# Eight turns of q and k moved from TensorE to DMA transposes, the last unit's halves in tiles of their own, and a new order of the steps

## The chip, the cores and the metric

One core of one Trainium2 chip. The time is the device time of one execution in microseconds (us). In what follows PE is the matrix engine (TensorE), DVE the vector engine, ACT the scalar engine, POOL GpSimd, and SP the engine that issues most DMAs. Every run has a state: it is called slow if it is more than 1.5% above the fastest run of the same kernel, and verdicts use only the other, fast, runs.

## The reference

Attention with a bias by distance, a local window of 96 keys and 8 global keys; then a feed-forward block on the result, whose nonlinearity is `h * softmax(h)` followed by a layer norm.

```python
# q, k, v: (4, 8, 768, 64); x: (3072, 512); w_in: (512, 1024); w_out: (1024, 512)
keep = is_global | ((rel >= 0) & (rel < 96))
scores = scale * q @ k.T - slope[h] * dist          # where keep, else -1e9
x = (softmax(scores) @ v)                           # heads side by side, 512 wide
h = x @ w_in
solu = h * softmax(h)
out = ((solu - mean) / sqrt(var + 1e-6) * g_ln) @ w_out
```

## The kernel before

The 3072 tokens are twelve units of 256 tokens (three per batch). For each unit, q and k are loaded, cast to 16 bits and turned, so that the head's 64 numbers lie on partitions; then come scores (`sc`, and `gs` for the global keys), exponentials (`pt`), sums (`lb`), values (`pa`), and the feed-forward block in two groups of 128 tokens: first layer (`ph`), exponential (`e`), product (`un`), a turn of `un` (mostly a DMA transpose, `uT`), second layer (`po`), scaling (`osb`), store. A list of steps, `ORDER`, fixes the order in which each engine gets its instructions; every engine works its own list in order, as the traces show (ACT stood for 2.21 us at one `osb` here, SP for 22.6 us at one transpose in experiment 2).

The turn of q and k, and the copy that puts the turned tile in token order:

```python
def small(shape, dt, name):                    # PSUM: two buffers for everything small
    return psum.tile(shape, dt, name=name, tag="small", bufs=2)

def turn(name, u):
    src = held.pop((name + "16", u))
    t = held["p" + name, u] = small([P, NR, P], FP16, name + "turned")
    for r in range(NR):                        # NR = 8
        nc.tensor.transpose(out=t[:, r], in_=src[:, r]..., identity=held["ident"])

def evac_qk(engine, name, u):
    t = held[name + "T", u] = attn.tile([P, NPAIR, UQ], FP16, name=name + "T", ...)
    cast(engine, t.rearrange("p g (i r) -> p g i r", r=NR),
         held.pop(("p" + name, u)).rearrange("p r (i g) -> p g i r", g=NPAIR))
```

The last unit's first layer is done in halves of the 1024 columns, and both halves are in one accumulator tile:

```python
def ff_in(t, h=None):
    if ("ph", t) not in held:
        held["ph", t] = big("ph")...           # one tile for both halves
    for j in range(NCC):
        for fh in (0, 1) if h is None else (h,):
            nc.tensor.matmul(out=held["ph", t][:, ts(fh, 512)], ...)
```

and the order near the end has `A:11:0:0 E:11:0:0 U:11:0:0 A:11:0:1 E:11:0:1`: A is the first layer, E the exponential, U the product. So the second half is written after the first half's readers.

The softmax here doesn't subtract the row's maximum and nothing guards it: scores larger than these inputs give would overflow.

## Time and profile before

| | before |
|---|---|
| median of the timed runs | 174.66 us (174.57 to 175.02) |
| span in the profile | 173.2 us |
| PE, DVE, ACT, POOL busy | 154.9, 127.3, 144.5, 91.4 us |
| moved by DMA | 34.35 MB |

The lines of the page that carry the argument are in the prediction below. These are the only two PE waits of over 0.1 us between 60 and 120 us (columns: engine, tile and line that waited, what it waited for, total us, times, longest):

```profile
PE gs L353 <- ACT osb L536: 1.3, 1, 1.3
PE ph L446 <- DVE xT L430: 0.7, 1, 0.7
```

### The profile page before, as it was taken

Reading aid. Unit: us, or ns where it says so; the run is one execution under the profiler, and the core shown is the slowest. Engines: PE = TensorE matmul, PEld = TensorE weight load, DVE = VectorE, ACT = ScalarE, POOL = GpSimd, SP = SyncE. Lnnn points to the kernel's source line nnn. Section 1 sums busy time; section 2 is a strip of 40 time slices with the busy share of each in tenths; the row PEclk is TensorE's granted clock in tenths of the full one; section 3 lists DMA queues with packets and bytes.
Section 4 is the critical chain, followed back from the end, with each engine's and each line's share of the span. In section 5 each row is a group of like instructions: output and inputs, shape, how many; then the busy total and the mean of one; then the engine's idle time right before and its main releaser. Section 6 shows DMA issues by size and latency. Waiting matters only on the chain.

```text
span 173.2 us, 4093 instructions
## 1 busy us (share of the span) xinstructions
PE 154.9 (89%) x1551; PEld 86.1 (50%) x1551; DVE 127.3 (73%) x200; ACT 144.5 (83%) x232; POOL 91.4 (53%) x195
## 2 busy tenths in 40 slices
PE   0179599899999989997999999999999958998997
PEld 0156375655654545436455655555545634454443
DVE  5079978999899989929989899869837672475310
ACT  5959999899999997769999899999895566796540
POOL 5276809300814998987288987882210001464760
PEclk9999759999999999999999999999999999999999
DMA  4999999999999998689999692398753530055354
GB/s 138 309 346 310 328 255 244 256 354 287 312 341 162 221 109 166 111 249 234 360 206 155 147 217 98 121 264 224 167 140 74 169 125 0 0 164 139 68 162 198
DMA packets 52532, 34.35 MB, mean 198 GB/s; under 512 B 43169, under 2 KB 43681, under 8 KB 52513
## 3 DMA queue, kind: packets, MB, share of 16 engines
q1 hardware_dynamic: 48784, 27.14, 63.9%
q0 software_dynamic: 1984, 5.77, 13.9%
q10 hardware_dynamic: 1744, 1.18, 2.5%
q8 instruction: 12, 0.20, 0.5%
q14 instruction: 8, 0.06, 0.1%
HBM read 23.07 MB, written 6.29 MB: 169 GB/s over the span
## 4 chain that ended last, share of the span: by engine, by line
PE 66%; POOL 10%; DVE 5%; DMA 5%; ACT 5%; issue 5%; SPq 4%; POOLq 0%; DVEq 0%; ACTq 0%
PE ph L446 21%; PE po L522 20%; PE lb L393 5%; PE pa L412 4%; PE warm L230 4%; SPq L157 4%; PE sc L324 3%; DMA q<-in_q_dram 3%; PE qturned L301 3%; POOL gw L594 2%; DMA v<-in_v_dram 2%; PE kturned L301 2%; DVE q L140 2%; ACT pt L333 2%; PE pa L422 1%
## 5 line engine op out<-in xcount | busy, mean ns | idle before, releaser
L446 PE MATMUL ph<-w_in,xT 128*128 128x512 f16 x192 | 44.9, 379 | 3.1 <-DVE un L468 2.3
L522 PE MATMUL po<-gw,uT 128*128 128x512 f16 x192 | 44.5, 379 | 0.0
L333 ACT ACTIVATE pt<-sc 128x896 f16<-128x896 f32 (+1 forms) x48 | 40.0, 871 | 2.2 <-PE sc L324 2.0
L468 DVE SCALAR_TENSOR_TENSOR un<-e,ph 128x1024 f16<-128x1024 f16 (+1 forms) x26 | 29.1, 1135 | 8.5 <-ACT e L460 7.6
L340 DVE TENSOR_TENSOR pt<-pt,mask 128x896 f16<-128x896 f16 (+1 forms) x48 | 28.3, 614 | 5.5 <-ACT pt L333 5.5
L446 PEld LDWEIGHTS <-xT 128*128 128x128 f16 x192 | 17.8, 98 | 24.0 <-issue 2.6
L460 ACT ACTIVATE e<-ph 128x1024 f16<-128x1024 f32 (+1 forms) x26 | 24.8, 955 | 4.5 <-PE ph L446 2.8
L522 PEld LDWEIGHTS <-uT 128*128 128x128 f16 x192 | 17.9, 98 | 20.9 <-issue 0.5
L477 ACT ACTIVATE sq<-un 128x1024 f16<-128x1024 f16 (+1 forms) x26 | 25.7, 990 | 2.0 <-DVE un L468 1.8
L497 POOL TENSOR_SCALAR w<-s,w 128x1 f32<-128x1 f32 x22 | 6.8, 311 | 32.3 <-ACT sq L477 30.6
L324 PE MATMUL sc<-qT,kT 64*128 64x128 f16 (+2 forms) x256 | 15.9, 246 | 3.0 <-ACT kT L138 1.8
L430 DVE TENSOR_TENSOR xT<-pa,rlb 128x1024 f16<-128x1024 f32 x12 | 14.6, 1221 | 2.9 <-ACT rlb L402 1.6
L301 PE MATMUL kturned<-ident,k 128*128 128x128 f16 x96 | 8.8, 246 | 8.0 <-POOL k L142 8.0
L495 POOL TENSOR_SCALAR w<-mean,w 128x1 f32<-128x1 f32 x24 | 14.5, 605 | 2.4
L499 POOL TENSOR_TENSOR rs<-w,neghalf 128x1 f32<-128x1 f32 x24 | 14.6, 610 | 2.0
L140 DVE COPY kT<-kturned 128x1024 f16<-128x1024 f16 x9 | 11.0, 1222 | 6.0 <-PE kturned L301 6.0
L534 DVE TENSOR_SCALAR osb<-po,rs 128x512 f32<-128x512 f32 (+1 forms) x15 | 10.7, 711 | 5.8 <-DMA out_dram<-osb 3.0
L401 ACT ACTIVATE rlb<-lb 128x1024 f32<-128x1024 f32 x12 | 12.4, 1032 | 3.0 <-PE lb L393 2.8
L536 ACT ACTIVATE osb<-po,rs 128x512 f32<-128x512 f32 (+1 forms) x11 | 7.1, 650 | 8.5 <-PE po L522 4.5
L324 PEld LDWEIGHTS <-kT 64*128 64x128 f16 x256 | 9.3, 100 | 8.3 <-issue 4.6
L402 ACT ACTIVATE rlb<-rlb 128x1024 f32<-128x1024 f32 x12 | 12.7, 1057 | 0.4
L301 PEld LDWEIGHTS <-k 128*128 128x128 f16 x96 | 7.1, 111 | 10.1 <-POOL k L142 8.2
(88 smaller groups left out, 230.2 us busy)
## 6 DMA issues: line engine op xcount, KB each, us to landing
out_dram<-osb SPq DMA_DIRECT2D x11, 512.0 KB, 2.9
q<-in_q_dram SPq DMA_DIRECT2D x19, 256.0 KB, 5.2
k<-in_k_dram SPq DMA_DIRECT2D x18, 256.0 KB, 5.3
v<-in_v_dram SPq DMA_DIRECT2D x16, 256.0 KB, 6.3
v<-in_v_dram POOLq DMA_DIRECT2D x7, 256.0 KB, 5.0
k<-in_k_dram POOLq DMA_DIRECT2D x6, 256.0 KB, 8.2
w_out<-in_moe_w_out_dram SPq DMA_DIRECT2D x3, 512.0 KB, 6.1
q<-in_q_dram POOLq DMA_DIRECT2D x5, 256.0 KB, 8.6
```

Of the source, the lines that this page charges most:

```text
L301: nc.tensor.transpose(out=t[:, r], in_=src[:, r].rearrange("p m d -> p (m d)"), identity=held["ident"])
L324: nc.tensor.matmul(out=sc[:, m, o : o + e - a], lhsT=held["kT", u - s + j // 2][r, g, ts(j % 2, P)], rhs=qT[r, g, a:e], start=True, stop=True,
L333: nc.scalar.activation(out=pt[:, :, 0:w], in_=held.pop(("sc", u, g))[:, :, 0:w], func=AF.Exp, scale=inv_sqrt_d)
L340: nc.vector.tensor_tensor(out=pt[:, :, 0:w], in0=pt[:, :, 0:w], in1=held["mask"][:, g, :, o : o + w], op=ALU.mult)
L430: nc.vector.tensor_tensor(out=xT.rearrange("p g (r i) -> p g r i", r=2), in0=held.pop(("pa", u)).rearrange("p g (i r) -> p g r i", r=2), i ...
L446: nc.tensor.matmul(out=held["ph", t][:, ts(fh, 512)], lhsT=held["xT", t[0]][:, j, ts(t[1], P)], rhs=held["w_in"][:, j, ts(fh, 512)], start ...
L460: nc.scalar.activation(out=held["e", t][:, f], in_=held["ph", t][:, f], func=AF.Exp, accum_out=s0)
L468: nc.vector.scalar_tensor_tensor(out=held["un", t][:, f], in0=held["e", t][:, f], scalar=1.0, in1=held["ph", t][:, f], op0=ALU.mult, op1=A ...
L477: nc.scalar.activation(out=sq[:, f], in_=held["un", t][:, f], func=AF.Square, accum_out=s2)
L495: eng.tensor_scalar(out=w2, in0=mean, scalar1=mean, scalar2=w1, op0=ALU.mult, op1=ALU.subtract)
L499: eng.tensor_tensor(out=rs, in0=w3, in1=held["neghalf"], op=ALU.pow)
L522: nc.tensor.matmul(out=held["po", t], lhsT=held["uT", t][:, c, :], rhs=held["gw"][:, c, :], start=(c == 0), stop=(c == NFC - 1),)
```

## The change

It has three parts. Five turns of k (units 7 to 11) and three of q (units 9 to 11) become DMA transposes, into SBUF tiles, with the copy into token order kept. The last unit's first layer is whole again, and the halves of its second layer (transposed piece, output) have their own tiles. The order of all steps was searched anew, and with it went choices of engine: for instance ACT has four copies of turned tiles and four output scalings fewer.

```diff
-NIN, NV = 13, 4
+NIN, NV, NTX = 13, 4, 2
 ORDER = """ ...                                   (all of it differs)
-... A:11:0:0 E:11:0:0 U:11:0:0 A:11:0:1 E:11:0:1 ...
+... A:11:0 O:6:1 o:D:6:1 E:11:0 U:11:0 ...        (whole)
-... ck:D:9 ... tk:9 ek:D:9 ...
+... ck:D:9 ... dk:S:9 ... ek:D:9 ...              (cast, DMA turn, copy; likewise the other seven)
+    def turn_dma(queue, name, u):
+        src = held.pop((name + "16", u))
+        t = held["p" + name, u] = attn.tile([P, NR, P], FP16, name=name + "x", tag="tx", bufs=NTX)
+        queues[queue].dma_start_transpose(out=t, in_=src.rearrange("p r m d -> p (r m d)"))
-    def ff_in(t, h=None): ...
+    def ff_in(t): ...                             (no halves; likewise exp, mul, square, stats)
     def ff_evac(engine, t, h=None):
-        held["uT", t] = ... (one tile, halves of it)
+        held["uT", t, h] = ... (a tile for each half); likewise osb in ff_scale
```

("..." marks cuts.)

## The prediction

> **What bounds the kernel now.** I read the page first (busy shares, slices), then the groups by shape, then a table of windows, then the chain in order of time for the last 37 us.
>
> ```profile
> PE 154.9 (89%) x1551; PEld 86.1 (50%) x1551; DVE 127.3 (73%) x200; ACT 144.5 (83%) x232; POOL 91.4 (53%) x195
> PE   0179599899999989997999999999999958998997
> PEclk9999759999999999999999999999999999999999
> DMA  4999999999999998689999692398753530055354
> ```
>
> The 89% of PE hides three stages. Up to slice 8 (about 35 us) PE has gaps and waits for loads and first casts; from there to slice 31 nearly every slice is 9; slice 32 shows a hole; the last stage is full again. The windows say the same in microseconds (columns: window, its length, then busy time and instructions of each engine, granted clock, DMA share, GB/s):
>
> ```profile
> 36.00:139.00 103.00, 100.78 (x1077) 54.80 (x1072) 86.46 (x131) 93.23 (x144) 58.89 (x111) 1.00 0.89 200
> 139.00:173.20 34.20, 30.47 (x176) 14.40 (x170) 13.87 (x27) 20.50 (x42) 13.53 (x43) 1.00 0.36 108
> ```
>
> In the middle 103 us PE is busy for 100.8, ACT for 93.2 and DVE for 86.5: PE sets the pace, ACT is 8 us behind it, DVE 14. So a microsecond of PE work taken out there should come off the end nearly whole, if the other two let it. The chain at the end (start, length, what):
>
> ```profile
> 139.38 1.03 ACT rlb L401
> 140.43 1.07 ACT rlb L402
> 141.52 0.04 DVE xT L430
> 141.56 1.11 issue
> 142.66 0.70 DVE un L468 x2
> 143.40 6.20 PE ph L446 x28
> ...
> 159.80 8.63 PE po L522 x40
> 168.44 3.88 PE warm L230 x18
> ```
>
> and the matmuls that stand behind 143.40, from the timeline:
>
> ```profile
> 143.40 6.20 PE L446 MATMUL ph<-w_in,xT 128*128 128x512 f16 x28 [2.34 <-DVE un L468]
> ```
>
> The reader is to see that the only large PE gap after 36 us is this 2.34 us, and what ends it: the product of the first half of the last unit's row (un). The second half of that row's first layer is written into the other half of the same accumulator tile, and in the program order it stands behind the half product that reads the tile. The wait is one on a shared tile, not on data. After it PE runs on to 168.44; the rest, 168.44 to 173.2, is the last scaling and the last store (the warm-up matmuls there only accompany it).
>
> The rows that price the change:
>
> ```profile
> L140 DVE COPY kT<-kturned 128x1024 f16<-128x1024 f16 x9 | 11.0, 1222 | 6.0 <-PE kturned L301 6.0
> L140 DVE COPY qT<-qturned 128x1024 f16<-128x1024 f16 x8 | 9.7, 1224 | 2.4 <-PE qturned L301 2.2
> L140 DVE CAST q<-q 128x1024 f16<-128x1024 f32 x9 | 7.1, 788 | 0.0
> L138 ACT ACTIVATE qT<-qturned 128x1024 f16<-128x1024 f16 x4 | 4.2, 1047 | 1.7 <-PE qturned L301 1.7
> uT<-un SPq DMA_TRANSPOSE x22, 3.6
> ```
>
> [...] a TensorE turn is recorded at 219 ns at the least, eight pipelined ones take 0.45 to 0.55 us of the chain, and a DMA transpose of eight blocks lands a median 3.6 us after its issue. It is slower, but on no compute engine. [...] 1222 ns for a copy out of PSUM, 788 for a cast of as many elements from SBUF. [...]
>
> **The change part by part.**
>
> Turns off PE. Eight turns (k of units 7 to 11, q of 9 to 11) leave PE, 64 matmuls with their weight loads; the instruction count on PE agrees. On the chain after 36 us there are eleven turns of 0.45, 0.55, 0.45, 0.46, 0.45, 0.55, 0.55, 0.45, 0.45, 0.45 and 0.45 us, mean 0.48. Eight times 0.48 is 3.8 us. Those that go are all in the saturated stage, so I count them in full: minus 3.8.
>
> The last unit. Its rows are no longer split in the first layer: whole ones again, with the second-layer halves (the transposed piece and the output) in tiles of their own. The shared accumulator wait goes. The new order also keeps two second-layer outputs of earlier units for the tail. By hand: behind the last attention product PE has six first-layer and ten second-layer groups of 1.73 us and 0.9 of turns, 28.6 us, against fourteen groups, 0.9 and the 2.34 wait, 27.5, before. The two extra groups are 3.5 us that the middle no longer carries. I see one new wait of about 0.5 us: the last transpose has to wait for a buffer that the second half of the last unit gives back, then about 3.1 us (as the last two took) while PE has two groups, 3.46 us, less what precedes. Minus 2.3, plus 0.5.
>
> DVE. Copies of turned tiles go from 17 to 21, of which 7 read SBUF. If these cost 0.75 (an estimate from the casts, 734 to 788 ns), 14 x 1.222 + 7 x 0.75 = 22.4 against 20.8: plus 1.6. One more cast, plus 0.75. Output scalings 13 to 17, 4 x 0.746: plus 3.0. Two w_out scalings less at 0.48: minus 1.0. Four half products of 0.77 with their accumulator reads become two of 1.30: minus 0.5. Sum plus 3.9: 131.2.
>
> ACT. Copies of turned tiles 7 to 3, 4 x 1.04: minus 4.2. Output scalings 9 to 5, 4 x 0.689: minus 2.8. One more cast plus 1.05, one more w_out scaling plus 0.7. Halves of exponentials and squares made whole: 3.15 to 2.45 and 3.28 to 2.5, minus 1.5. Sum minus 6.7: 137.8.
>
> POOL. Two casts less (minus 2.1), one scaling more (1.0), the sums of halves gone (1.0), six more load issues (5 x 0.6 + 1.04, 4.0): about plus 1.9, on an engine half idle.
>
> DMA. Eight more transposes at 1.24 us of SP's queue: 10 us on a queue that mostly waits. They run at about 75 to 115 us, in part where the DMA row is still 9.
>
> The start. q of unit 0 is now fetched and turned first, cast on ACT; three loads are issued from ACT. Before, the first scores began at 11.67. After, by the spacing of landings (first casts could start at 6.9 and 8.4 with four and five loads issued), q's cast about 6, its turn 7, k's cast 8, its turn 9, its copy until about 11.2. That is 0.3 us sooner, within what I can tell; minus 0.3.
>
> Middle check. Without the turns PE needs about 97 us of a stage then about 99 long; DVE would have about 90.5 there and ACT about 88. Three engines at 89 to 98% in queues that run in order: some of the saving will come back as small waits. I put 1.6 us on it, guided by the 2.2 us that PE idles between 36 and 139 now.
>
> Sum: 174.66 - 3.8 - 2.3 + 0.5 - 0.3 + 1.6 = 170.4.
>
> **The rivals.** First, DVE takes PE's place: it gains 3.9 us just where it is 84% busy (86.5 of 103). For it: 3.9 us more makes that 90.4 of some 99, and the new copies have to wait for a DMA. Against it: ACT is relieved by more than DVE is loaded, so work waiting for ACT (5.5 us of DVE's waits are for exponentials) comes sooner. It would give back 2 to 3 us: 172 to 173. Second, the transposes collide with loads: SP issues in order, and a transpose that waits for its cast holds the loads behind it; old transposes took up to 10.1 us to land. For it: DMA is full until about 104 us. Against: the order places each well ahead of its copy, and no DMA wait of the middle is on the old chain. It would cost 1 to 3 us: 171 to 173. Third, the early stage decides: the new order was chosen as a whole, and before 35 us PE waits for loads and runs at a granted clock of 0.65 between 17.3 and 26. A better or worse start moves all by 1 to 2 us: 168.5 to 172. Fourth, the saving is hidden because something else ends the kernel; against this the chain is PE from 36 to 168 but for the one hole. That would leave 174.
>
> **Range and chances.** The two counted savings are 6.1 us. If three quarters of them are given back, the time is about 173.2; if nothing is given back and the start is a microsecond better, it is 174.66 - 6.1 - 1.0 = 167.6, near enough the low end. Predicted 170.4, range 167.8 to 173.2. The line for faster by over 2% is 171.17, so the centre is 0.8 below it with a spread of about 2: faster 0.63, same 0.35, slower 0.02.
>
> **What would show it.** PE should have 64 fewer matmuls and some 4 to 5 us less busy time; the 2.34 us wait for un should be gone and no PE wait over 1 us stand after 130 us. Copies of the tiles turned by DMA should last about 0.75 us on DVE; if they last 1.2, DVE has 3 us more and the first rival gains. DVE should be near 131 busy, ACT near 138. PE waits for DVE copies of kT or qT, or DVE waits for the transposes, between 75 and 115 us would show the first or the second rival. First scores later than 12.5 us, or a first-layer group of unit 0 later than about 36 us, would show the third. The prediction fails if the middle has more than 4 us of PE idle time.

## More of the kernel before

The two small PSUM buffers are shared: `qturned`, `kturned`, `gs`, `po`, `lT` and some others take turns in them.

`gs` is computed from qT and a tile of global keys; it does not read `osb`. It waits 1.34 us for `osb` because ACT, when it writes `osb`, frees the small PSUM buffer that `gs` is to be written into. And ACT comes to it late because it works its list in order and an earlier item, another `osb`, had waited for a statistic that POOL computes (`rs`).

That item in ACT's list, then the chain of waits that ended last (start, length, what):

```profile
74.95 0.69 ACT L536 ACTIVATE osb<-po,rs 128x512 f32<-128x512 f32 x1 [2.21 <-POOL rs L499]
```

```profile
56.22 0.46 PE qturned L301 x8
...
74.36 0.57 POOL rs L499
...
78.29 0.59 ACT osb L536
78.92 0.20 PE gs L353 x4
```

So between 56.7 and 78.9 us the chain does not run over PE at all.

## The result, and the profile after

The changed kernel took 170.48 us (median of four runs: 170.78, 170.18, 169.48, and 176.19), beside 174.62 for the kernel before on the same chip. The ratio of the fast runs is 0.974, with a 95% interval of 0.969 to 0.979: faster by 2.6%. Ratios here and below are the mean time of one kernel's fast runs over that of the other kernel's fast runs of the same rounds, so they are not quite the ratio of the medians.

The head of the page of the changed kernel: busy time of each engine, then tenths of busy time in 40 slices of the span.

```profile
PE 151.6 (90%) x1487; PEld 81.6 (48%) x1487; DVE 132.0 (78%) x203; ACT 140.0 (83%) x218; POOL 100.3 (59%) x194
PE   0248988889999999999799998999999999999897
...
DMA  4999899999999999799999999599979509365753
```

The slice that showed the hole near 140 us is gone, and the weak slices are now spread: one before 80 us, one about 100. The windows, as before (window, length, busy time and instructions of PE, weight loads, DVE, ACT, POOL, granted clock, DMA share, GB/s), now split where it matters. First the kernel before:

```profile
60.00:80.00 20.00, 17.83 (x166) 9.13 (x168) 15.34 (x25) 16.85 (x30) 17.85 (x29) 1.00 0.93 166
80.00:120.00 40.00, 40.00 (x446) 22.15 (x444) 35.89 (x52) 38.76 (x59) 29.25 (x63) 1.00 0.88 202
```

and the changed one, with its whole middle added:

```profile
60.00:80.00 20.00, 20.00 (x209) 10.38 (x208) 19.08 (x30) 19.44 (x33) 18.51 (x28) 1.00 1.03 201
80.00:120.00 40.00, 38.27 (x373) 19.34 (x371) 36.20 (x52) 37.24 (x58) 31.77 (x52) 1.00 1.02 229
...
36.00:139.00 103.00, 100.95 (x1059) 53.55 (x1057) 92.98 (x138) 95.52 (x148) 69.72 (x118) 1.00 0.97 220
```

Read them against each other. From 60 to 80 us PE had been idle for 2.17 us, the two waits shown earlier; now it is never idle. From 80 to 120 us PE had never been idle; now, with the turns gone, it is idle for 1.73 us. So the idle time of the whole middle is about as large as before (103 - 100.95 = 2.05 us, against 2.22), but it lies elsewhere.

How far PE got with the work that both kernels have can be counted from the trace: every matmul by its columns (216 ns for 512, as eight took 1.73 us; those that run side by side, as four `gs` of 256 columns that took 0.29 us together and not 0.43, at their share), turns and warm-ups left out, up to a given time. The lead of the changed kernel over the one before, in us of PE work:

| up to | 36 us | 60 | 80 | 120 | 139 | 144 | 155 | 163 |
|---|---|---|---|---|---|---|---|---|
| lead | -0.4 | -0.3 | +2.4 | +2.7 | +2.7 | +5.4 | +5.2 | +4.5 |

Start -0.4; 36 to 139 us +3.1, of which 2.7 come between 60 and 80; the hole +2.7; the tail -0.9. Of the thirteen turns after 36 us eight are gone: four became three before 60 us, two became one between 60 and 80, and seven became one between 80 and 120. So six of the eight, 2.9 us of PE time, left a stretch in which the lead grew by 0.3. (By busy time it is 2.9 - 1.73 = 1.2; ends of matmuls are modelled, and the two counts differ by up to a microsecond.) Between 60 and 80 us, with one turn fewer, it grew by 2.7: that is the idle time of 2.17 us filled, and a turn.

In this stretch the chain of the changed kernel does not run over PE either. It comes from POOL again, which here issues a load of q behind its statistics:

```profile
73.99 0.80 POOL rs L490
74.79 1.36 POOL k L157
76.15 4.22 DMA q<-in_q_dram
...
83.15 1.90 PE ph L450 x8
```

ACT no longer waits for POOL there. Over the whole span 48% of the chain is PE's, where it was 66%.

The copies, by shape (line, engine, tiles, count, busy us, mean ns), show that the size of one estimate did not hold:

```profile
L140 DVE COPY kT<-kturned 128x1024 f16<-128x1024 f16 x5 | 6.1, 1218 | 1.9 <-PE kturned L301 1.8
L140 DVE COPY kT<-kx 128x1024 f16<-128x1024 f16 x4 | 4.8, 1200 | 0.0
L140 DVE COPY qT<-qx 128x1024 f16<-128x1024 f16 x3 | 3.6, 1200 | 0.0
L138 ACT ACTIVATE kT<-kx 128x1024 f16<-128x1024 f16 x1 | 2.0, 2004 | 0.0
...
kx<-k SPq DMA_TRANSPOSE x5, 4.9
qx<-q SPq DMA_TRANSPOSE x3, 3.8
```

A copy of a tile in SBUF (kx, qx) takes DVE 1200 ns, as one out of PSUM (1218), and takes ACT 2004 ns, twice what one out of PSUM took it before (1031). In this profile no copy by DVE waited for a transpose (0.0 idle before), so 3.8 to 4.9 us from issue to landing lay beside other work.

The end, from the chain of waits (start, length, what):

```profile
155.56 2.30 PE po L512 x11
157.86 4.13 DMA uT<-un
```

and the same stretch from PE's own list, with the idle time ahead of a group and its releaser in brackets:

```profile
159.82 1.90 PE L512 MATMUL po<-gw,uT 128*128 128x512 f16 x8 [0.80 <-DMA uT<-un]
162.04 1.90 PE L512 MATMUL po<-gw,uT 128*128 128x512 f16 x8 [0.32 <-DMA uT<-un]
```

The last two transposes are not there when PE is: 0.80 and 0.32 us. PE's last useful group ends at 163.94 us instead of 168.44. What comes after it (scaling and last store) is 5.06 us instead of 4.76.

### The profile page after: what moved, and what is told of

The parts are those of the page before. It is cut to its first block, busy times and chain, and to the rows that moved or that the text cites.

```text
span 169.0 us, 3944 instructions
## 1 busy us (share of the span) xinstructions
PE 151.6 (90%) x1487; PEld 81.6 (48%) x1487; DVE 132.0 (78%) x203; ACT 140.0 (83%) x218; POOL 100.3 (59%) x194
## 4 chain that ended last, share of the span: by engine, by line
PE 48%; ACT 18%; DMA 14%; POOL 10%; issue 6%; DVE 2%; SPq 1%; DVEq 0%; POOLq 0%; ACTq 0%
PE po L512 17%; PE ph L450 16%; DMA q<-in_q_dram 5%; ACT pt L338 4%; PE lb L398 4%; DMA v<-in_v_dram 4%; ACT e L462 3%; PE warm L230 3%; PE sc L329 2%; ACT sq L475 2%; DMA uT<-un 2%; DMA k<-in_k_dram 2%; PE pa L417 2%; ACT rlb L406 2%; POOL gw L588 2%
## 5 line engine op out<-in xcount | busy, mean ns | idle before, releaser
L467 DVE SCALAR_TENSOR_TENSOR un<-e,ph 128x1024 f16<-128x1024 f16 x24 | 29.0, 1218 | 6.4 <-ACT e L462 4.6
L462 ACT ACTIVATE e<-ph 128x1024 f16<-128x1024 f32 x24 | 24.5, 1021 | 7.9 <-PE ph L450 7.6
L475 ACT ACTIVATE sq<-un 128x1024 f16<-128x1024 f16 x24 | 25.4, 1059 | 2.5 <-DVE un L467 2.0
L488 POOL TENSOR_SCALAR w<-s,w 128x1 f32<-128x1 f32 x24 | 9.9, 414 | 17.7 <-ACT sq L475 15.9
L527 DVE TENSOR_SCALAR osb<-po,rs 128x512 f32<-128x512 f32 x17 | 12.7, 748 | 8.5 <-PE po L512 8.5
L483 POOL TENSOR_SCALAR w<-s 128x1 f32<-128x1 f32 x24 | 14.1, 586 | 2.5 <-ACT e L462 0.4
L140 DVE COPY qT<-qturned 128x1024 f16<-128x1024 f16 x9 | 11.0, 1220 | 5.3 <-PE qturned L301 5.3
L486 POOL TENSOR_SCALAR w<-mean,w 128x1 f32<-128x1 f32 x24 | 11.6, 483 | 2.4
L301 PE MATMUL qturned<-ident,q 128*128 128x128 f16 x72 | 6.6, 250 | 7.0 <-POOL hm L242 6.6
L417 PE MATMUL pa<-pt,v 128*64 128x128 f16 (+2 forms) x256 | 10.9, 232 | 0.0
```

What stands on the lines that cost most here:

```text
L417: nc.tensor.matmul(out=po[m * D : m * D + D, g, a:e], lhsT=held["v16", u - s + j // 2][:, 2 * g + m, j % 2], rhs=pt[:, m, o : o + e - a], ...
L462: nc.scalar.activation(out=held["e", t], in_=held["ph", t], func=AF.Exp, accum_out=s0)
L467: nc.vector.scalar_tensor_tensor(out=held["un", t], in0=held["e", t], scalar=1.0, in1=held["ph", t], op0=ALU.mult, op1=ALU.mult, accum_out=s1,
L475: nc.scalar.activation(out=sq, in_=held["un", t], func=AF.Square, accum_out=s2)
```

## The experiments

All in fours on one chip beside the kernel before; "before" is the median of the 11 runs there: 175.08 us for the first four, 175.96 for the next four, 175.89 for the last four. On the last two chips the kernel before itself has two levels, about 174.5 and 176.3 us, all but one of the 22 runs (177.02) called fast; that widens the intervals.

### 1. The accumulator wait alone

One step moved in the kernel before: the second half of the first layer ahead of the exponential and product that read the first half.

```diff
-A:11:0:0 E:11:0:0 U:11:0:0 A:11:0:1 E:11:0:1
+A:11:0:0 A:11:0:1 E:11:0:0 U:11:0:0 E:11:0:1
```

> The kernel before with one step moved: the second half of the last unit's first layer is multiplied before the half product that reads the same accumulator tile, so PE no longer waits for it. My theory: the 2.34 us hole at 141 us closes and PE runs on, 174.6 - 2.3 = 172.3 us (ratio 0.987). Rival (the hole only moves, because ACT and DVE are as late as PE there): 173.8 to 174.6, with a new PE wait of 1 to 2 us after 140 us.

Measured: 172.74 us (172.42 to 173.09), ratio 0.9857 (0.9825 to 0.9888). In PE's list the first layer is one piece where there had been two and a hole:

```profile
139.64 7.08 PE L446 MATMUL ph<-w_in,xT 128*128 128x512 f16 x32
```

So the hole was on the path that sets the end, and closing it pays 1.43%, or 2.5 us of 175.08. One step of the list gives over half of the whole gain.

### 2. and 3. The DMA turns alone, in the old order

The kernel before with the eight turns issued from SP, each right behind its cast; then the same with the step of experiment 1. Four buffers for the turned tiles, so that those are not what is short.

```diff
+NTX = 4
-... ck:D:8 ... tk:8 ek:A:8 ...
+... ck:D:8 dk:S:8 ... ek:A:8 ...       (likewise k7, k9 to k11, q9 to q11)
```

> The kernel before, its order kept, with the eight turns (k of units 7 to 11, q of 9 to 11) done by DMA transposes issued right after each cast, and nothing else. My theory (PE sets the pace between 36 and 139 us, so PE work taken out comes off the end): 64 matmuls gone, 3.8 us, 170.8 us if no new wait arises (ratio 0.978), up to 172 with small waits. Rival (the turns pay only in the new order, because a transpose takes 3.6 us and more to land and holds up SP's queue): 173 to 176, with waits of DVE or ACT for the transposes and then of PE for kT and qT.

> Both edits on the kernel before, its order otherwise kept. Theory: the two add, 174.6 - 2.3 - 3.8 = 168.5 us at best (ratio 0.965), about 169.5 with small waits; then the new order as a whole has added nothing. Rival (the gain of the changed kernel needs the searched order): 171.5 to 174.

Measured: 202.48 us, with fast runs of 198.69 and 201.55, ratio 1.142 (1.133 to 1.151); and 198.16 us, ratio 1.131 (1.127 to 1.136). With the hole closed 14.2% becomes 13.1%, which goes the way of experiment 1, though the intervals touch; the loss is from the transposes. SP's list in the first of the two, then the longest wait of SP's queue, then one of ACT and three of PE:

```profile
49.13 2.65 SPq L521 DMA_TRANSPOSE uT<-un  x1
73.28 1.23 SPq L307 DMA_TRANSPOSE kx<-k  x1
74.56 1.33 SPq L521 DMA_TRANSPOSE uT<-un  x1
```

```profile
SPq L307 <- DVE un L473: 23.4, 2, 22.6
```

```profile
ACT kT L138 <- DMA kx<-k: 5.7, 1, 5.7
```

```profile
PE pa L417 <- DVE v L140: 6.5, 1, 6.5
PE lb L389 <- DVE un L473: 6.4, 2, 5.9
PE po L527 <- DMA uT<-un: 6.1, 3, 5.1
```

SP issues nothing between 51.8 and 73.3 us. Its next item is the transpose of k7 (line 307), which waits for its cast. That cast is an instruction of DVE, which also works in order and gets to it at 72.57 us; the wait of 22.6 us is put down to the DVE instruction that came last by the profile (`un`). Behind the waiting transpose stand loads of v and old transposes, and PE then waits for those. The transposes themselves landed in 3.1 to 4.4 us. This is the second rival of the prediction: the issue that waited for 22.6 us held back everything behind it in SP's queue.

Two more things are in the loss. ACT's copy of k8 waits 5.7 us for a transpose that has been issued (at 42.23 us) and not landed; the exponentials stand behind it in ACT's list, and PE waits 5.9 us for what comes of them. And the granted clock is 0.93 over these executions, 0.80 between 80 and 100 us, where the kernel before has 0.98 to 1.00. PE is busy for 158.8 us, and for 151.6 in the changed kernel, which has the same number of matmuls: by that estimate some 7 of the 25 us lost are longer matmuls (eight of 512 columns from 90.91 us on took 3.60 us, where elsewhere they take 1.90). What lowered the clock is not shown, and the three parts are not separated.

In the changed kernel SP's queue still waits for such transposes, but for 8.6 us at the longest, and they stand where what is behind them is not needed yet: between 60 and 139 us no PE group there waits for a DMA.

### 4. The changed kernel with its turns back on PE

```diff
-dk:S:7 ek:D:7
+tk:7 ek:D:7                             (likewise the other seven, right ahead of the copy)
```

> The changed kernel with its eight DMA turns put back on PE, each just ahead of its copy, the order otherwise kept. Theory: the 3.8 us come back, about 174.3 us (ratio to before 0.998). Rival (the order made the gain, not the turns): 170.5 to 171.5. PE busy time should rise by about 4 us; DVE should stay near 132, as its copies from SBUF were found to take 1.20 us, the same as from PSUM.

Measured: 179.07 us, fast runs 177.1 to 179.25 (two slow ones at 183 and 190), ratio 1.016 (1.010 to 1.022). Against the changed kernel's ratio, 0.974 here and 0.967 on another chip (experiment 12), that is 4.2 to 4.9%, some 7.3 to 8.6 us. Eight turns of 0.48 us of PE are 3.8 (by busy time PE has 2.9 us more, 154.5 against 151.6). PE's list has more:

```profile
96.02 0.29 PE L357 MATMUL gs<-qT,kgz 128*32 128x256 f16 x4 [1.40 <-ACT osb L528]
...
101.14 0.61 PE L300 MATMUL kturned<-ident,k 128*128 128x128 f16 x8 [0.29 <-ACT pg L365]
102.86 0.61 PE L300 MATMUL qturned<-ident,q 128*128 128x128 f16 x8 [1.12 <-ACT kT L137]
...
112.37 0.61 PE L300 MATMUL kturned<-ident,k 128*128 128x128 f16 x8 [0.68 <-DVE osb L526]
114.03 1.89 PE L511 MATMUL po<-gw,uT 128*128 128x512 f16 x8 [0.37 <-DVE qT L139]
```

None of these five groups reads what it is said to wait for: a turn of q has no use for kT, an output none for qT. They wait for one of the two small PSUM buffers, which an evacuation of another tile frees. Together 1.40 + 0.29 + 1.12 + 0.68 + 0.37 = 3.86 us, and 3.8 + 3.9 = 7.7 is within what was measured. So in the new order a turn by DMA saves two things: PE's time, and a stay of the turned tile in a PSUM buffer. The prediction had only the first. It is a comparison within an order that was searched without these turns, so it does not say that the kernel before paid as much for its buffers.

### 5. The kernel before with the turns cut to an eighth

Each of the eight late turns does one of its eight matmuls, and the copy reads that piece eight times. PE's work falls by 56 matmuls; the PSUM buffers, the copies and the order stay. Its output is wrong, which doesn't matter for the time.

```diff
-for r in range(NR):
+for r in range(1 if late else NR):
     nc.tensor.transpose(out=t[:, r], ...)
```

> Wrong result on purpose. The kernel before, with order, buffers, queues and copies as they are, but each of the eight late turns does one of its eight matmuls, so 56 of the 64 matmuls that the change takes off PE are gone and nothing takes their place. If PE sets the pace there, as I said, 7/8 of 3.8 us come off: 3.3 us, ratio 0.981. Rival (ACT or DVE is the true bound of the middle and PE only follows): 0 to 1 us, ratio 0.994 to 1.0, with PE idle instead.

Measured: 175.66 us beside 175.96, ratio 0.9994 (0.9938 to 1.0051). Seven eighths of 3.8 us are 3.3, which would have been a ratio of 0.981; that is outside the interval, which allows 1.1 us at the most. The windows of its profile, and one of the new waits:

```profile
60.00:80.00 20.00, 17.54 (x165) 8.86 (x163) 15.44 (x25) 16.93 (x31) 17.83 (x29) 1.00 0.69 155
80.00:120.00 40.00, 38.87 (x407) 20.27 (x404) 36.51 (x54) 39.11 (x61) 29.13 (x63) 1.00 0.90 209
```

```profile
103.51 1.89 PE L454 MATMUL ph<-w_in,xT 128*128 128x512 f16 x8 [0.80 <-ACT pt L341]
```

PE is idle for 1.13 us where it never was, and waits for an exponential by ACT, which is busy for 39.11 of the 40 us (38.76 in the kernel before). Between 60 and 80 us the old idle time is still there (2.46 us). By the count of leads PE gets ahead of the kernel before by 0.9 us between 80 and 120 us, so about a third of the 3.3 may come off, which is within the rival's 0 to 1 us. In the old order, then, the saturated stretch was not PE's alone, and most of what PE gains it waits away. That ACT is what holds it besides is argued from its 97% and this wait, not shown; experiments 9 and 10 try it.

### 6. The changed kernel with PE work added

64 matmuls of 128 columns, of no use, ahead of the scores of units 7 to 11, in tiles that are there anyway: about as much PE time as the turns took, and no PSUM buffer.

```diff
 sc = held["sc", u, g] = big("sc")
+if g == 0 and u >= 7:
+    for _ in range(8 if u < 9 else 16):
+        nc.tensor.matmul(out=sc[:, 0, 0:P], lhsT=held["ident"], rhs=held["ident"], ...)
```

> The changed kernel with 64 matmuls of 128 columns with their weight loads put back on PE as dummies, written into the score tile of the late units just before the scores overwrite it, so no buffer, copy or queue changes. If the PE time of the turns is what they cost, 3.6 to 3.8 us come back: 174.2 us, ratio to before 0.996. If the changed kernel's middle has slack on PE (it shows 2.6 us of idle PE between 78 and 112 us), 1 to 3 us. Putting the real turns back cost 8.6 us, so the part above what this run costs is waits for the turned tiles and PSUM buffers, not PE time.

Measured: fast runs 173.46, 175.23 and 175.37, ratio 0.9949 (0.9876 to 1.0022); three slow runs of 177.6 to 186.9. Against 0.974 (or 0.967) that is 2.1 (2.8) %, or 3.7 (4.9) us, for 64 x 54 ns = 3.5 us of PE time (54 ns is an estimate, a quarter of the 216 for 512 columns; eight turns of 128 columns took 0.45 us of the chain, 56 ns each). So in the new order PE work that is added costs about its length or more; with both intervals, anything from some 2 to 7 us is possible (an estimate), and two of the three fast runs lie 1.8 us above the third. That isn't the same as saying that work taken out was gained in full: by the table of leads it was not. The interval is wide, and its profile fell on a slow run, so no wait in it is read here.

### 7. The tail

In the changed kernel, the last rows' first layer moved ahead, and a fourth buffer for the transposed tile, so that the last transposes start sooner.

```diff
-name="uT", tag="uT", bufs=3
+name="uT", tag="uT", bufs=4
-O:10:0 ... A:9:1 ... E:9:1 ... U:9:1
+A:9:1 E:9:1 O:10:0 ... U:9:1 O:11:1:0
```

> The changed kernel with the last first-layer group of unit 9 one group earlier, its exponential and product moved with it, and four in place of three buffers for the transposed pieces. PE now waits 0.80 and 0.32 us for the last two transposes; if these waits are all that stands there, 1.1 us come off: ratio to before about 0.967. Rival (the last transposes are issued late because of SP's queue or the last product, so the wait stays): within 0.3 us of the changed kernel.

Measured: only two of six runs were fast, 171.16 and 173.21; ratio 0.981 (0.972 to 0.990). That overlaps the changed kernel's interval and does not decide. The profile does show that the waits for the DMA are gone; what remains is a wait of a turn for `osb`, a PSUM buffer again:

```profile
157.04 0.38 PE L495 MATMUL lT<-ident,un 128*128 128x128 f16 x4 [0.60 <-ACT osb L528]
157.26 7.07 PE L511 MATMUL po<-gw,uT 128*128 128x512 f16 x32
```

PE's last useful group ends 0.4 us later than in the changed kernel, since PE comes into the tail later in this run. Whether the 1.1 us of the tail can be had stays open.

### 8. What sets the time of the copies

In the changed kernel three of the copies out of SBUF get other patterns. Copy k8 is straight, k9 reads straight and writes scattered, q10 reads in steps of 4 elements and writes in steps of 8; the others are as they were. Its output is wrong, which doesn't matter for the time.

```diff
+if (name, u) == ("k", 8):  cast(engine, t "p (g i)", src "p (r i)")
+elif (name, u) == ("k", 9): cast(engine, t "p r i g", src "p r i g")
+elif (name, u) == ("q", 10): cast(engine, t "p g r i", src "p g r i")
```

> Wrong result on purpose (k of unit 8 is not put in token order). The changed kernel, one look, with three of the copies from SBUF in other loop orders: k8 straight through, k9 read straight and written scattered, q10 with an innermost step of 4 elements in and 8 out; the others as they are (innermost read step 128, write step 1), which took 1.20 us where I had estimated 0.75. If the step of the reading is what costs, k8 takes about 0.4 to 0.5 us and k9 about 0.75; if any SBUF copy of 2-byte elements in this kernel takes 1.2 us, k8 does too.

Measured, from DVE's and ACT's lists (k7, k8, k9, q10, then k10 on ACT); the single run took 177.8 us and is not used for a time:

```profile
71.64 1.08 DVE L140 COPY kT<-kx 128x1024 f16<-128x1024 f16 x1 [1.50 <-DMA kx<-k]
75.73 0.42 DVE L140 COPY kT<-kx 128x1024 f16<-128x1024 f16 x1
...
96.69 2.64 DVE L140 COPY kT<-kx 128x1024 f16<-128x1024 f16 x1 [0.63 <-DMA kx<-k]
105.41 2.51 DVE L140 COPY qT<-qx 128x1024 f16<-128x1024 f16 x1
```

```profile
105.05 2.08 ACT L138 ACTIVATE kT<-kx 128x1024 f16<-128x1024 f16 x1
```

Straight 0.42 us, as it is 1.1 to 1.3, written in steps 2.5 to 2.6. The pattern sets it. The copy into token order reads every 128th element (256 bytes apart) and writes side by side, and gains nothing on DVE from having its source in SBUF (1200 ns, 1218 from PSUM). In this run two of the copies do wait for their transposes, 1.50 and 0.63 us.

### 9. and 10. ACT relieved in the old order, without and with the turns cut

If ACT holds the old middle beside PE, relieving it should let the turns pay. Four copies and four scalings go from ACT to DVE, as in the change; then the cut of experiment 5 in addition (wrong).

```diff
-eq:A:7  ek:A:8  eq:A:10  ek:A:10  o:A:0:0  o:A:1:0  o:A:0:1  o:A:5:0
+eq:D:7  ek:D:8  eq:D:10  ek:D:10  o:D:0:0  o:D:1:0  o:D:0:1  o:D:5:0
```

> The kernel before in its own order, with four copies of turned tiles (q7, k8, q10, k10) and four output scalings moved from ACT to DVE, as the change does: ACT -7.0 us (4 x 1.04 and 4 x 0.69), DVE +7.9 (4 x 1.22, 4 x 0.75). If ACT alone held the middle of the kernel before, 172.5 to 173.5 (ratio about 0.99). If PE and ACT hold it together, relieving one alone gives about nothing: 174 to 176 (0.995 to 1.005). If DVE then becomes the bound: over 176.

> Wrong on purpose: the previous run plus the cut turns of the earlier run (each late turn does one of its eight matmuls). Theory 'PE and ACT together hold the middle, so that relieving both is what pays': 171.5 to 172.5 (ratio 0.982 to 0.988), as the middle of the changed kernel gained about 3 us. Rival 'only the newly searched order pays for it': like either of the two alone, 174 to 176 (0.995 to 1.005).

Measured: 178.10 us, ratio 1.011 (1.006 to 1.017); and 176.43 us, ratio 1.0035 (0.9976 to 1.0094). Relieving ACT alone costs 1.1%; at 178 us that is the third case of its expectation, in which DVE becomes the bound. With it the cut turns pay 1.0114 - 1.0035 = 0.8%, 1.4 us of the 3.3, which is not clear of noise, as the intervals overlap. The theory that relieving both is what pays has fallen: it wanted 0.982 to 0.988. Two windows and the longest PE waits of the second kernel:

```profile
60.00:80.00 20.00, 18.41 (x162) 8.98 (x162) 19.44 (x30) 16.11 (x29) 17.19 (x30) 1.00 0.57 151
80.00:120.00 40.00, 37.23 (x398) 19.71 (x391) 36.48 (x53) 35.03 (x53) 29.31 (x63) 1.00 0.92 197
```

```profile
PE ph L454 <- DVE xT L438: 1.6, 3, 1.0
PE po L530 <- DVE osb L542: 0.8, 1, 0.8
PE qturned L302 <- DVE osb L542: 0.7, 1, 0.7
```

All three waits are for DVE, two of them for a PSUM buffer that DVE frees (`osb`). DVE is full between 60 and 80 us in both kernels (19.44 of 20, where the kernel before has 15.34) and at 91% (36.48 of 40) between 80 and 120, where PE is idle for 2.8 us. So the old order had no room on DVE for ACT's work at this place: by these numbers DVE had taken over as the bound there, and the two runs do not settle whether ACT was the second bound before. Neither the turns nor this division of work gave the middle's gain in the old order. What is left is the new order, or the PSUM buffers, which neither of the two runs set free.

### 11. The score matmuls read the turned q directly

A version that might beat both: the three copies of q are left out, and the scores of units 9 to 11 read the DMA's tile with a strided moving operand.

```diff
-rhs=qT[r, g, a:e]                       # 16-bit elements side by side
+rhs=qT[r, g, a // NR : e // NR, :]      # 8 elements 256 bytes apart, then 4 elements on
```

> The changed kernel without the copies of q of units 9 to 11: the score matmuls read the turned tile in SBUF directly, through a strided moving operand. It takes 3 x 1.20 us from DVE. If the copies in token order lie beside PE's work and DVE is not the bound: within 0.6 us of the changed kernel run beside it. If DVE co-paces the middle: 1 to 2 us faster, 168.5 to 169.5 (ratio about 0.966). If TensorE reads a strided moving operand more slowly: score matmuls of units 9 to 11 longer than those of unit 8, and the time 1 to 3 us longer.

Measured: fast runs 176.02 and 175.82, four slow ones; ratio 1.002 (0.993 to 1.010), some 6 us behind the changed kernel's fast runs beside it. The row of the widest score matmuls of the changed kernel (all units), then of this one:

```profile
L329 PE MATMUL sc<-qT,kT 64*128 64x224 f16 x96 | 13.0, 282 | 2.2 <-DVE kT L140 1.3 <-DVE qT L140 0.5 <-ACT pt L338 0.3
```

```profile
L333 PE MATMUL sc<-qT,kT 64*128 64x224 f16 x96 | 16.5, 348 | 2.4 <-DVE kT L139 1.7 <-DVE qT L139 0.3 <-ACT pt L342 0.3
```

Only a quarter of the row are strided ones, so the mean hides their size. Taken apart in the trace, the 128 score matmuls of all shapes before those of units 9 to 11 (from 32 us on) last 229 ns in the mean in both kernels. The 64 of units 9 to 11 stay at 229 in the changed one and take 438 here; those of 224 columns take 553 where they took 258. So the copy into token order, which looks like waste, saves PE more than it costs DVE (209 ns in each of the 64, against three copies of 1.20 us). The profile fell on a slow run; the lengths of single matmuls at a granted clock of 1.00 are read from it, no waits.

### 12. The changed kernel again

> The changed kernel again, unaltered, beside these three on one chip: fast runs 169.5 to 171, ratio 0.969 to 0.979. A ratio above 0.985, or more slow runs than the kernel before has, would show that the gain depends on the chip, or that this order scatters more.

Measured: eight runs, three at 169.60 to 170.09 and five at 172.88 to 173.85 (called slow by the rule of 1.5%, at a mean granted clock of 0.99 to 1.00, the fast ones at 1.00); ratio of the fast runs 0.967 (0.959 to 0.975). The median of all eight is 173.19, beside 175.89 for all of before: 0.985. So the gain holds on a second chip, but this order has a level 3.5 us higher, into which over half of the runs fell there; the kernel before has one 1.8 us higher. More generally every kernel with the new order had runs at 175 us or above, or at such a higher level. Why is not known, and no difference that only those runs show is explained here. One place to look: in the profile of such a run the load of q that POOL issues lands later, DVE's cast waits 3.92 us for it (0.93 in the fast profile) and PE 2.14 us for its turn (0.39), and the granted clock is 0.91 between 80 and 100 us. Whether this is cause or consequence is open.

## Why the prediction was right or wrong

The time was right (170.4 against 170.48), and the mechanism it gave first, the hole at 141 us, is shown. Of the other terms several were off, and the total came out because their errors cancel: that 170.4 was so near is luck. By its steps:

**The hole, -2.3.** Right: -2.7 by the table of leads, and experiment 1 alone measured -2.5.

**Eight turns off PE, -3.8, "in full".** This is the step that failed. PE's count fell by 64, as said. But that PE alone holds the saturated stage, so that removed work comes off the end, does not hold for the kernel it was said of: in experiment 5 the removal of 3.3 us of it moved the time by 1.1 us at the most, with ACT at 97% in that stretch. Nor does the changed kernel's own trace show it: where six of the eight turns left, PE's other work got ahead by 0.3 to 1.2 us of 2.9.

**Small waits coming back, +1.6.** In kind right: 1.73 us of new idle time at 80 to 120 us. But in exchange the new order removed the two old waits at 60 to 80 us, 2.1 us, of which the prediction said nothing. It had the number 2.2 for the idle time of the middle, and used it only as a guide for what would come back. Against its fourth rival it even said that the chain is PE from 36 to 168 us but for the one hole. That reading is wrong: from 56.7 to 78.9 us the chain runs over DVE, ACT and POOL's statistics (it was also why only eleven of the thirteen turns stood on it), and the wait of 1.34 us is where it comes back to PE. Together the middle was put at -3.8 + 1.6 = -2.2 and gave -3.1, mostly in a place where the prediction had not looked.

**The new wait in the tail, +0.5.** It is there, in two pieces of 0.80 and 0.32; in leads the tail is +0.9. And what follows PE's last group is 0.3 longer.

**The start, -0.3.** Wrong in sign. The first scores start at 12.00 us, not 11.67, and the first layer of unit 0 at 37.19 instead of 36.20. Part of that is a different order there: by the table of leads it is +0.4. Its own sign for this rival, a first layer of unit 0 later than about 36 us, could not tell, since the kernel before was at 36.20 already.

With measured terms: +0.4 - 3.1 - 2.7 + 0.9 + 0.3 = -4.2, which is the change of the span. The prediction had -4.3, so it was too cautious by 1.3 us (0.9 in the middle, 0.4 at the hole) and too hopeful by 1.4 (0.7 at the start, 0.7 at the end), and the two cancel.

**The engines.** DVE was put at 131.2 and took 132.0, although the step under it was wrong: seven copies from SBUF, put at 0.75 us, took 1.20, which is 7 x 0.45 = 3.2 us more, so other items together came out 2.4 lower, above all the 48 mask products, which took 26.9 us instead of 28.8, and the casts, which took 686 to 714 ns each instead of 734 to 788. The prediction had kept the old costs. Why they were shorter was not tested. The estimate was carried over from casts whose pattern has runs of 64 elements; experiment 8 shows that the pattern sets the time. Nor do 1222 ns for a copy out of PSUM against 788 for a cast from SBUF show a price of the source in PSUM: the same pattern read from SBUF takes 1200. ACT was put at 137.8 and took 140.0, of which 1.0 is its one copy from SBUF at 2.0 instead of 1.03. POOL was put at +1.9 and took +8.9, mostly longer times of the same small instructions (`w<-s` 586 ns instead of 348); not tested. It was passed over as an engine half idle, but it stands on the chain of both kernels (at 61 to 75 us before, at 57 to 76 us after). PE's busy time fell by 3.3 us, not by 4 to 5.

**The rivals.** The first (DVE takes PE's place) did not come in the changed kernel, but it is what experiments 9 and 10 ran into. The second (the transposes hold up others) is real: it is in the 14% of experiment 2, with ACT's wait and the lower clock, and the new order, with the same eight transposes, does not have it. The third (the start) was small. The fourth (the saving is hidden) is what happens to most of the turns' time in the old order.

**What stays open.** How much of the two waits at 60 to 80 us went because turned tiles no longer sit in PSUM, and how much because steps were merely moved, is not separated. A third cause is untested: the longer of the two stood behind ACT's wait of 2.21 us for POOL's `rs`, which the changed kernel does not have. Experiment 5 left the buffers as they were, so it cannot tell; a kernel in the old order in which the late turns take neither PE time nor a PSUM buffer would. The higher level of the changed kernel is open too.

## What to carry to other kernels

That an engine is busy all through a stage does not show that its removed work comes off the end: look at the next one in that very window (here ACT, 97%), and at whether the chain runs over the engine there, before counting in full. Follow a wait back past its releaser: the one of 1.34 us for ACT led to POOL. When a wait's releaser is a tile that the waiting instruction never reads, look for a wait for a buffer, as here (1.34 us in the kernel before, 0.29 to 1.40 us in experiment 4): an operation that stays out of that buffer can save this as well as its own time (3.9 and 3.8 us there, by the estimate of experiment 4). A DMA that waits belongs behind what it could hold up: the same eight transposes are what made the kernel 14% longer where loads stood behind them and an ACT copy right after, and in the fast profile of the changed kernel no copy waited for one.
